# A state-space scan stepped in pairs: 28 of 42 complex rotations taken out of TensorE, two matrices more in their place, and a new order of all instructions

## Chip, cores and metric

One core of one Trainium2 chip. The metric is the time of one execution on the device in microseconds (us); lower is better. The core's engines run beside each other and meet at semaphores: PE (TensorE, matrix products), DVE (VectorE), ACT (ScalarE), POOL (GpSimd) and SP (SyncE, which here issues the DMAs). Each of them works through its own queue in order.

## The reference, cut to what matters

Two independent blocks on 2048 positions of width 448, their outputs set side by side. Block A is attention with 16 heads over a window of 8 positions at a distance of 2; block B is a diagonal complex state model:

```python
qkv = x @ wqkv                                    # A: q, k, v; 16 heads of 28
logits = einsum(q, k[pos - 2*w], w = 0..7) * scale   # masked below position 0
a = einsum(softmax(logits), v[pos - 2*w]) @ wo
...
Lam_bar = exp(exp(log_dt) * Lam)                  # B: 448 complex states
Bu = x @ (((Lam_bar - 1) / Lam)[:, None] * Bmat).T
for t in range(L):
    h = Lam_bar * h + Bu[t]                       # the scan over 2048 steps
y = 2 * real(h_all @ Cmat.T) + x * Dskip
```

## The kernel before

**State of block B.** The 448 complex states lie as 7 groups `g` of 64, real parts on partitions 0 to 63 and imaginary parts on 64 to 127. So a multiplication by a power of `Lam_bar` is a matmul with a 128x128 matrix, a *rotation*: `R[:, g, k]` (built by `rb(k)` on DVE) turns by power k + 1. The 2048 steps are T = 4 residues `j` of 512 chunks, the chunks again even and odd (256 each).

**Steps of block B.** `BU` (line 672) projects x with the transposed B matrix `BT` into a PSUM bank for each (g, j). `BR` (685) adds the state one step earlier, rotated by one power, for j = 1, 2, 3: 21 rotations of 512 columns. `z` (689) evicts each bank to `Z` (for j = 3 the even half to `Z3`); `UP` (697) turns the even half of j = 3 by four steps onto the odd one, and `y` evicts it. `sa`, `sb`, `sd` (716 to 734) scan over the 256 pairs of chunks, on DVE, for two groups at a time (0 and 1, 2 and 3, 4 and 5, 6): turn by tables `tab`, one real scan, turn back. `DN` (737) and `dn` (742) give the even chunks from the odd ones. `H_(j, g)` (748) rotates the state at the chunk's start by j + 1 steps, for j = 0, 1, 2: 21 rotations of 512 columns; `h(j, g)` (755) adds each to `Z`, on DVE from PSUM. `C(j, ct)` (766) then makes a block of 128 output rows: 7 matmuls, one for each g, with `Cw`; `c` (774) adds `x * Dskip`, `oc` stores. The block (j, ct) = (2, 3) is made in two halves, `CH`, `ch`, `oh`. `ca` (ACT) and `cs` (DVE) scale `Cw`; `rk` holds magnitudes.

**Steps of block A.** `XI`, `XA`, `XH` transpose x on PE and `xa`, `xh` evict; `QK`, `QS` (326 to 341) make q and k and `qk`, `qh` evict; `V_`, `v` make v. `P(u, r, ws)` (line 368) multiplies q by four shifted copies of k on DVE, 28 products of 2048 columns; `E_` sums over the head's columns on PE; `lt`, `TR`, `tr`, `sma`, `smb`, `smc` are the softmax; `AL`, `al`, `ad`, `sp` spread the probabilities into bands `PT` through DRAM; `AV`, `av` apply them to v; `W_`, `w`, `ow` are the output projection.

**Who evicts.** The helper `evict` (line 113) takes a PSUM bank to SBUF on ACT where the step in the order ends in ".", and on DVE where it ends in "=". So groups on line 113 hold evictions of many steps; they are told apart by their tiles.

**Order.** Nothing reorders at run time. The string `ORDER` (line 32) is a list of 557 steps; "BU201@12" is the step `BU` with arguments 2, 0, 1 that takes PSUM banks 1 and 2. The loop at line 849 emits the steps in this order, so it is the order on each engine's queue at once, SP's included. The loads of x, `wq` and B at lines 139 to 178 are issued on SP before the list. `WU`, 24 matmuls on zeros and a first `Exp` on ACT, stands second in the list; `BD`, the DMA transposition of B, first. Ahead of the list DVE clears some tiles (lines 116, 224, 226).

Of the kernel before, what the change touches and what calls it, by code (L numbers as in the profile page):

```python
# [17 lines left out]
T = 4  # L18
# [8 lines left out]
SHR = 1.0 - 1e-6  # L27
MAGIC = 12582912.0
# [4 lines left out]
BD WU@0 XI0@12 XI1 xa00= xa01. PP@3 pcopy pa pb pd_ xh0. QS00@4 XH1@5 pc ty5 ty4 pe qk000. pf XA10@6 tf4 tf5 xt1 ts04  # L33
xh1= XA11@7 xa11= xt3 QS10@0 QK021@13 qk010. QK061@24 xa10= QK060 QK020 ts05 pg qh011. QS01@5 qk001. P001 QS11@7
qk020= ts15 qh000. QK041@60 ts25 ty0 QK031@15 P000 qk021. QK030 rb2 tf0 qk030. P020 P021 ts14 QK040 V_100@31 qk011.
P011 qk031. qk041. qh001. ts24 QK050@75 QK051 V_011@02 ts00 ty1 qh010. qk050. V_010 E_00@4 E_02 qk040. tf1 P010 E_01@7
# [26 lines left out]
def kernel(  # L63
# [820 lines left out]
```

## Time and profile before

| | |
|---|---|
| time of the runs shown | median 135.06 us of 3 (134.78 to 135.12) |
| span of the profiled execution, first to last instruction | 132.7 us |
| median less span | 2.3 us |
| busy PE / DVE / ACT / POOL | 125.4 / 116.9 / 89.7 / 19.8 us |
| instructions PE / DVE / ACT | 1068 / 211 / 180 |
| matmuls of `BR` (line 686), 512 columns | 6.3 us in all (20 recorded) |
| matmuls of `H_` (line 752), 512 columns | 6.7 us in all (21) |

The profile gives no time of its own for the profiled execution beyond its span; what lies around the span is taken as the 2.3 us by which the median of the runs exceeds it. A matmul's duration includes its drain, which overlaps the next one; so what a matmul costs in a run of matmuls is the distance from start to start, well below its duration. The same holds for DVE and ACT to a lesser degree. L242 in a row is line 242 of the kernel before. In a timeline or the chain of work the first number is the start and the second the extent, both in us from the span's start; "x3" joins three neighbours. In a table of windows each engine's entry is its busy time in the window, with instructions in brackets.

### The profile page before, as it was taken

How to read it: one execution, taken by the hardware profiler on the slowest of the kernel's cores; microseconds unless marked ns; L12 is line 12 of the kernel's file. 1: busy time of each engine (PE TensorE's matmuls, PEld its weight loads, DVE VectorE, ACT ScalarE, POOL GpSimd, SP SyncE). 2: the span in 40 equal slices, each digit the busy share in tenths (PEclk: the TensorE clock that was granted, in tenths of full speed). 3: DMA queues.
4: the chain of work that ended last, by engine and by line, in shares of the span. 5: the costliest groups of instructions: out<-in, count | busy, mean ns of one | idle time of the engine just before them, and what ended most of it. 6: DMA issues, size and time to landing. Idle time of an engine off the chain costs nothing.

```text
span 132.7 us, 2860 instructions
## 1 busy us (share of the span) xinstructions
PE 125.4 (94%) x1068; PEld 63.4 (48%) x1078; DVE 116.9 (88%) x211; ACT 89.7 (68%) x180; POOL 19.8 (15%) x37
## 2 busy tenths in 40 slices
PE   6987999999999999999999999999999999999990
PEld 6642344344333533435335645955954455555550
DVE  5589999999899999999999798999999996969851
ACT  3396499994578999999899899999999110100000
POOL 6801000000000000035599700000000000000000
PEclk9999999999999999999999999999999999999998
DMA  4897998999989998997849599895513301321543
GB/s 109 201 228 159 304 241 147 152 200 212 263 187 214 208 224 215 380 180 134 223 148 185 199 172 373 187 182 70 175 35 110 104 0 38 105 69 39 182 153 110
DMA packets 45348, 22.62 MB, mean 170 GB/s; under 512 B 33239, under 2 KB 44311, under 8 KB 45335
## 3 DMA queue, kind: packets, MB, share of 16 engines
q1 hardware_dynamic: 45272, 22.45, 73.3%
q8 instruction: 8, 0.13, 0.4%
q14 instruction: 5, 0.04, 0.1%
q10 hardware_dynamic: 63, 0.01, 0.0%
HBM read 11.68 MB, written 6.29 MB: 135 GB/s over the span
## 4 chain that ended last, share of the span: by engine, by line
PE 64%; ACT 15%; DVE 9%; SPq 5%; issue 3%; DMA 2%; POOL 0%
PE ps L242 31%; PE ps L771 14%; PE ps L686 4%; PE ps L380 3%; PE ps L752 3%; SPq L131 2%; ACT ctmp L648 2%; ACT oT L113 2%; SPq L137 2%; ACT kf L113 2%; PE ps L511 2%; DMA wq<-in_A_wqkv_dram 2%; PE ps L498 2%; ACT qf L113 2%; DVE hs L727 1%
## 5 line engine op out<-in xcount | busy, mean ns | idle before, releaser
L368 DVE TENSOR_TENSOR pr<-qf,kf 128x2048 bf16<-128x2048 bf16 x24 | 28.3, 1217 | 0.2 <-ACT kf L113 0.2
L242 PE MATMUL ps<-xbuf,BT 128*128 128x512 bf16 (+1 forms) x108 | 23.1, 379 | 0.7 <-issue 0.6
L242 PE MATMUL ps<-xT,wq 128*128 128x512 bf16 (+1 forms) x92 | 20.9, 380 | 1.4 <-DVE xT L113 0.5
L771 PE MATMUL ps<-Cw,Z 128*128 128x448 bf16 x105 | 21.3, 352 | 0.2
L113 ACT CAST Z<-ps 128x512 bf16<-128x512 f32 (+1 forms) x32 | 15.2, 509 | 1.0 <-PE ps L242 0.6
L113 ACT CAST ya<-ps 128x448 bf16<-128x448 f32 (+1 forms) x14 | 7.3, 547 | 11.5 <-issue 10.9
L771 PEld LDWEIGHTS <-Z 128*128 128x128 bf16 x105 | 10.3, 98 | 10.1 <-issue 0.7
L242 PEld LDWEIGHTS <-BT 128*128 128x128 bf16 (+1 forms) x112 | 8.8, 97 | 12.3 <-issue 3.3
L511 PE MATMUL ps<-wo,oT 128*128 128x448 bf16 x64 | 13.8, 353 | 0.2 <-DVE oT L113 0.2
L242 PEld LDWEIGHTS <-wq 128*128 128x128 bf16 (+1 forms) x96 | 7.6, 97 | 13.1 <-issue 4.0
L757 DVE TENSOR_TENSOR Z<-ps,Z 128x512 bf16<-128x512 f32 x21 | 13.5, 680 | 0.4 <-PE ps L752 0.3
L777 DVE TENSOR_TENSOR xbuf<-ps,xnB 128x448 bf16<-128x448 f32 x15 | 8.9, 619 | 4.6 <-PE ps L771 3.8
L242 PE MATMUL ps<-wq,xT 128*128 128x448 bf16 (+1 forms) x64 | 12.1, 353 | 0.0
L841 POOL MEMSET PT<- 128x4320 f32 x3 | 11.1, 3728 | 1.7 <-ACT Z L113 1.7
L113 ACT CAST kf<-ps 128x512 bf16<-128x512 f32 x12 | 6.9, 593 | 4.0 <-PE ps L242 3.9
L648 ACT ACTIVATE ctmp<-Cw,c2t 64x448 f32<-64x448 bf16 x14 | 9.3, 666 | 0.3
L113 ACT CAST oT<-ps 128x512 bf16<-128x512 f32 x16 | 9.0, 614 | 0.1
L511 PEld LDWEIGHTS <-oT 128*128 128x128 bf16 x64 | 6.1, 98 | 6.1 <-DVE oT L113 0.7
L498 PE MATMUL ps<-PT,v_s 128*32 128x135 bf16 (+1 forms) x256 | 8.3, 298 | 0.0
L242 PEld LDWEIGHTS <-xT 128*128 128x128 bf16 (+1 forms) x64 | 5.0, 97 | 6.4 <-issue 2.6
L498 PEld LDWEIGHTS <-v_s 128*32 128x32 bf16 x256 | 7.0, 112 | 0.4 <-issue 0.4
L113 ACT CAST v_s<-ps 128x448 bf16<-128x448 f32 x14 | 7.0, 549 | 0.0
(153 smaller groups left out, 191.1 us busy)
## 6 DMA issues: line engine op xcount, KB each, us to landing
PT<-pd SPq DMA_DIRECT2D x16, 156.0 KB, 4.0
xnB<-in_B_x_dram SPq DMA_DIRECT2D x2, 896.0 KB
out_dram<-ya SPq DMA_DIRECT2D x16, 112.0 KB, 1.8
out_dram<-xbuf SPq DMA_DIRECT2D x15, 112.0 KB, 1.8
pd<-Ak SPq DMA_DIRECT2D x2, 640.0 KB, 3.7
xbuf<-in_A_x_dram SPq DMA_DIRECT2D x2, 448.0 KB
xnB<-in_B_x_dram SPq DMA_DIRECT2D x4, 224.0 KB, 7.0
xnB<-in_B_x_dram SPq DMA_DIRECT2D x4, 192.0 KB, 4.6
```

The costliest lines, as they stand in the source:

```text
L113: (ACT.copy if e == "A" else V.tensor_copy)(o, i)
L242: PE.matmul(o, l, r, start=(first and i == 0), stop=(not first and i == len(pairs) - 1 and not more[s]))
L368: V.tensor_tensor(t[:], q.unsqueeze(1).to_broadcast((128, 4, 512)), k4, ALU.mult)
L380: PE.matmul(acc[s][32 * i:32 * i + 32], E[:, f, ws, :], t[:, i, :], start=(f == 0 and ws == 0), stop=False)
L498: PE.matmul(p[32 * hh:32 * hh + 32, 128 * bl:128 * bl + n], v_s[:, t, 4 * hg + hh, :], PT[:, t % NS, (4 * hg + hh) // HS, (4 * hg + hh) % ...
L511: PE.matmul(p[:, 0:D], late["oT"][:, b // 4, hg, par, 128 * (b % 4):128 * (b % 4) + 128], late["wo"][:, hg, :], start=(hg == 0), stop=(hg ...
L648: ACT.activation(t[a:a + 64, 0:D], Cw[b:b + 64, g, :], ACTF.Copy, scale=c2t[a:a + 64, g:g + 1])
L686: PE.matmul(pp["z", g, j][:], rot(g, 0), late["Z"][:, g, j - 1, :], start=False, stop=True)
L757: V.tensor_tensor(zz, pp.pop(("h", j, g))[:], zz, ALU.add)
L771: PE.matmul(p[:, 0:D], z, Cw[:, g, :], start=(g == 0), stop=(g == G - 1))
L777: V.tensor_tensor(yo, pp.pop(("c", j, ct))[:, 0:D], xnB[:, ct, j, :], ALU.add)
L841: POOL.memset(late["PT"][:, 4 * i:4 * i + 4].rearrange("p t g n -> p (t g n)").bitcast(F32), 0.0)
```

## The change

Steps now go in pairs (j = 0, 1 and j = 2, 3). The second step of a pair isn't advanced but kept *turned back* by one power: its x is projected with a matrix of its own, `BT[1]` = B turned back by one power, and accumulates onto the first step's sum in the same PSUM bank. What is read out for it is then multiplied with an own output matrix, `Cw[1]` = C turned forward by one power. So within a pair no rotation is needed; `BR` is left once for each group (from pair 0 to pair 1, by two powers), and `H_` once for each group, whose result `h` adds to both steps of the first pair at once.

- New on PE: `BB` (4 matmuls of 128 columns for each group) and `CB` (one of 448) make the two matrices, and ACT evicts them (`bb`, `cb`). `BT[1]` is written in place over `Bn`, once `BD` has read it; `Cw[1]` takes the place of `BT[0]`.
- `BF` and `BX`/`BY` replace `BU`: three full matmuls, and the half-height rest, one for each step. A pair shares a bank, so the second step's matmuls wait for the first step's eviction `z`.
- `DO` and `do` give j = 2 the odd chunks' share beside `DN`'s; `H_` is evicted to SBUF (`hs`), and `h` is one addition of 2 x 512 columns there.
- `R` has three matrices, and the third is first the turn back (`rb2`), then the turn forward (`rb3`). The scans work in place in `Z3`. `w` evicts to the upper half of `xbuf`, in 8 slots where there were 6; `al(3)` uses `Ak0` a second time.
- `ORDER` is new throughout (580 steps) and gives many evictions to another engine: on DVE now 2 `al`, 2 `av`, 2 `ci`, 1 `hs`, 1 `tr`, 6 `z`, 3 `qk`, 2 `v`, 1 `w`, 2 `xa`, 1 `xh`; before 1 `av`, 3 `z`, 3 `qk`, 2 `v`, 3 `w`, 3 `xa`, 1 `xh`. `WU` goes from the second place to the end; `LC`, the loads of C, from behind the four `xt` to ahead of `BD`.

The order's start, its first products, the stretch around the last scan, and its end:

```diff
-BD WU@0 XI0@12 XI1 xa00= xa01. PP@3 pcopy pa pb pd_ xh0. QS00@4 XH1@5 pc ty5 ty4 pe qk000. pf XA10@6 tf4 tf5 xt1 ts04
-xh1= XA11@7 xa11= xt3 QS10@0 QK021@13 qk010. QK061@24 xa10= QK060 QK020 ts05 pg qh011. QS01@5 qk001. P001 QS11@7
...
-sb6 W_41@4 w41. cs2 W_50@7 H_03@5 sd6 DN5@3 dn5 W_60@1 ow31 ca5 W_70@2 ow30 ow41 w60. ow71 h13 cs5 H_11@4 C33@3 w00.
...
-oc10 oc01 oc22 c02 ow51 oc02 CH1@7 ch1 oh1
+XI0@01 XI1 xh0= xa00. PP@2 xa01= QS10@3 pcopy pa XH1@4 xh1. XA10@5 XA11@6 pb QS00@7 xa11. pd_ QK021@01 QK041@24 xa10=
+LC pe ty4 tf4 ty0 QK020 pc qk020= QK040 tf0 QK050@65 qk000. QS11@7 qk040= qk010. QK051 QK031@30 QK030 P001 P000 qk041.
+pf QS01@4 ts04 qk050. V_111@26 ts00 qk051= qk021. qk030. ts10 QK061@51 BD P041 P040 QK060 V_110 P020 qk011. ts20 P021
...
+rb3 AL2@5 cs0 sa0 ts12 z41. ts03 UP2 BF410@6 pm2 pm0 cs6 z51= xd1 sp0 AL3@1 BF611 BR4 BF311 CB6@3 BR5 ts22 al3= ca4
+y2. BX3141 sp1 al2. ts13 BX6151 z63. z33. cb6. AV020@1 sb0 AV000@2 av020. AV011@5 av011. sd0 z42= AV001@3 xd0 z52=
...
+cs5 W_20@2 av100. dn2 DO2 av120. cb0. cb1. H_0@6 sb4 w30. CB5@0 ow11 hs0. W_40@4 w40. CB2@5 sd4 cb2. xd2 W_61@7 W_70@6
+DN3@4 CB3@5 ow00 ow30 ts26 ow31 w61. do2 w70. DN5@3 sa6 dn3 dn5 ow70 sb6 W_51@7 W_41@6 ow10 DO3 w20. do0 H_3@2 cb3.
+sd6 h0 cb5. hs3. ow61 W_60@5 w41. DN4@0 DO5 w60. C32@1 dn4 DN6@2 W_21@6 ow20 do5 w21. do3 dn6 c32 H_2@5 W_50@3 w51.
+DO4 h3 hs2. ow40 DO6 do6 H_5@4 xd3 H_4@6 C31@7 h2 c31 ow41 do4 hs5. hs4. w50= ow21 H_6@1 h5 W_71@5 h4 C33@2 oc31 C21@4
+C22@7 c33 hs6. CH0@6 ch0 h6 C20@0 oc33 c22 CH1@3 C13@1 w71. c20 C10@5 oc32 ch1 C12@2 c21 C03@6 c13 oc21 oh1 ow50 oh0
+c10 oc20 oc10 C00@7 C02@0 oc22 C01@3 c00 c03 c02 C11@4 oc13 oc03 c12 C30@1 oc00 c01 ow60 oc01 WU@5 c11 oc12 c30 oc02
+ow71 oc11 ow51 oc30
```

The steps that are new or changed:

```diff
-    Bn = s2.tile([128, G, 512], BF16, tag="Bn")
+    Bn = keep.tile([128, G, 512], BF16, tag="Bn")
...
-    BT = keep.tile([128, G, 4, 128], BF16, tag="BT")
-    R = keep.tile([128, G, T, 2, 64], BF16, tag="R")
-    Cw = keep.tile([128, G, D], BF16, tag="Cw")
+    BT = [keep.tile([128, G, 4, 128], BF16, tag="BT", name="BT"), Bn.rearrange("p g (f n) -> p g f n", f=4)]
+    R = keep.tile([128, G, 3, 2, 64], BF16, tag="R")
+    Cw = [keep.tile([128, G, D], BF16, tag="Cw", name="Cw"),
+          BT[0].rearrange("p g f n -> p (g f n)")[:, 0:G * D].rearrange("p (g d) -> p g d", g=G)]
...
-    def BR(g, j):
-        PE.matmul(pp["z", g, j][:], rot(g, 0), late["Z"][:, g, j - 1, :], start=False, stop=True)
+    def BB(g):
+        p = pp["bb", g] = ps()
+        for f in range(4):
+            PE.matmul(p[:, 128 * f:128 * f + 128], Bn[:, g, 128 * f:128 * f + 128], rot(g, BACK), start=(f == 0), stop=True,
+                      skip_group_check=True)
+    def bb(g, e):
+        evict(e, BT[1][:, g].rearrange("p f n -> p (f n)"), pp.pop(("bb", g))[:])
+    def CB(g):
+        p = pp["cb", g] = ps()
+        PE.matmul(p[:, 0:D], rot(g, FWD), Cw[0][:, g, :], start=True, stop=True)
+    def cb(g, e):
+        evict(e, Cw[1][:, g, :], pp.pop(("cb", g))[:, 0:D])
...
+    def BF(g, q, s):
+        p, new = zbank(g, q)
+        for f in range(3):
+            PE.matmul(p[:], BT[s][:, g, f, :], xTB[:, q, 4 * s + f, :], start=(new and f == 0), stop=True, skip_group_check=True)
+    def bhalf(g, q, s):
+        p, new = zbank(g, q)
+        r = slice(64 * s, 64 * s + 64)
+        PE.matmul(p[:], BT[s][r, g, 3, :], xTB[r, q, 3, :], start=new, stop=True, skip_group_check=True)
+    def BX(g, q, h, r):
+        bhalf(h, r, 0)
+        bhalf(g, q, 1)
+    def BY(g, q, s):
+        bhalf(g, q, s)
+    def BR(g):
+        p, new = zbank(g, 1)
+        PE.matmul(p[:], rot(g, R2), late["Z"][:, g, 1, :], start=new, stop=True, skip_group_check=True)
...
+    def DO(g):
+        PE.matmul(pp["dn", g][:, N2:], rot(g, R4), late["Z3"][:, g, EV:EV + N2], start=False, stop=True, skip_group_check=True)
+    def do(g):
+        zz = late["Z"][:, g, 2, :]
+        V.tensor_tensor(zz, pp.pop(("dn", g))[:], zz, ALU.add)
-    def H_(j, g):
-        p = pp["h", j, g] = ps()
+    def H_(g):
+        p = pp["h", g] = ps()
...
-    def h(j, g):
-        zz = late["Z"][:, g, j, :]
-        V.tensor_tensor(zz, pp.pop(("h", j, g))[:], zz, ALU.add)
+    def hs(g, e):
+        t = pp["hs", g] = late["sc"].tile([128, NC], BF16, tag="hp", name="hp", bufs=2)
+        evict(e, t[:], pp.pop(("h", g))[:])
+    def h(g):
+        zz = late["Z"][:, g, 0:2, :]
+        V.tensor_tensor(zz, pp.pop(("hs", g))[:].unsqueeze(1).to_broadcast((128, 2, NC)), zz, ALU.add)
...
-            PE.matmul(p[:, 0:D], z, Cw[:, g, :], start=(g == 0), stop=(g == G - 1))
+            PE.matmul(p[:, 0:D], z, Cw[j % 2][:, g, :], start=(g == 0), stop=(g == G - 1))
```

More of the change, by code (lines that the diff above doesn't have):

```diff
@@ L27 @@
 SHR = 1.0 - 1e-6
+FLOOR = 32.0
+R2, R4, BACK, FWD = 0, 1, 2, 2
 MAGIC = 12582912.0
 ORDER = """
[L33 to L36 removed]
```

138 lines of the change are left out of this document (72 added, 66 removed).

## The prediction

> **What bounds the kernel now.** I read the page's first lines and its forty slices, then a table of windows cut where the work changes, then the groups of instructions by shape.
>
> ```profile
> span 132.7 us, 2860 instructions
> ...
> PE   6987999999999999999999999999999999999990
> PEld 6642344344333533435335645955954455555550
> DVE  5589999999899999999999798999999996969851
> ```
>
> PE is full from the fifth slice to the last but one. But DVE is nearly as full until the 31st slice (103 us), and only then has air. The windows give the size:
>
> ```profile
> 14.06:48.00 33.94, 33.57 (x227) 13.67 (x229) 32.75 (x38) 27.03 (x58) 0.00 (x0) 1.00 1.10 212
> 48.00:72.00 24.00, 23.52 (x191) 10.16 (x194) 23.30 (x34) 23.14 (x42) 10.64 (x7) 1.00 0.85 214
> 72.00:102.10 30.10, 29.67 (x426) 18.51 (x427) 27.70 (x60) 28.84 (x58) 3.66 (x2) 1.00 0.71 171
> 102.10:129.65 27.55, 27.31 (x149) 14.24 (x146) 22.46 (x39) 2.32 (x5) 0.00 (x0) 1.00 0.27 86
> ```
>
> Behind the length stand busy PE, weight loads, DVE and ACT. The cuts at 14.06 and 102.10 are DVE's first product `P` and the end of its last scan group `sd6`:
>
> ```profile
> 11.69 0.18 DVE L580 TENSOR_TENSOR co<-cs,rk 128x28 f32<-128x28 f32 x1
> ...
> 14.06 1.22 DVE L368 TENSOR_TENSOR pr<-qf,kf 128x2048 bf16<-128x2048 bf16 x1
> ...
> 101.80 0.29 DVE L734 TENSOR_TENSOR Z<-vv,p 128x256 bf16<-128x256 bf16 x1
> ```
>
> Between these cuts DVE works 32.75 + 23.30 + 27.70 = 83.75 us of 88.04 and is idle 4.3. So two engines bind at once: PE over the whole span, and DVE up to `sd6`. The output stage (`C`, L771) can't begin before the scans are nearly through.
>
> **The change on PE.** Pitches (start to start) come from the chain's pieces, extent over count, and from one run of equal matmuls in the timeline, extent less a duration of 0.22 (L398, the same shape, is a row of 219 ns) over count less one:
>
> ```profile
> 80.21 0.12 PE ps L739
> 80.33 0.65 PE ps L686 x3
> ...
> 107.81 1.32 PE ps L771 x7
> ```
> ```profile
> 8.22 0.84 PE L294 MATMUL ps<-ident,xbuf 128*128 128x128 bf16 x12
> ```
> ```profile
> L398 PE MATMUL ps<-ident,lt 128*128 128x128 bf16 x16 | 1.2, 219 | 0.0
> ```
>
> So 256 columns take 0.11 to 0.12 us, 512 take 0.216, 448 take 0.189, 128 take 0.056. Removed: 14 of the 21 `BR` (L686) and 14 of the 21 `H_` (L752), 28 x 0.216 = 6.05. Added: `BB`, 28 of 128 columns, 1.57; `CB`, 7 of 448, 1.32; `DO`, 7 of 256, 0.76; the halves of B that no longer run two by two (`BY411`, `BY511`, both on the same half of the rows), 0.43. Net 2.0 us less. Changes of matmul shape in PE's order are about as many as before (42 against 44), and `C` is unchanged.
>
> Where the 2.0 lies matters. Ahead of its first `C`, PE loses 14 `BR` and 4 `H_` (3.9 us) and gains 3.9 of the 4.1 us of new work, so it comes there no sooner than now, at about 102.5. Behind it stand 10 `H_` fewer: 2.2 us.
>
> ```profile
> 102.48 1.73 PE L771 MATMUL ps<-Cw,Z 128*128 128x448 bf16 x7
> ```
>
> **The change on DVE.** In total it evens out: 21 additions `h` from PSUM become 7 `do` from PSUM and 7 wider `h` from SBUF, and the new order gives DVE more evictions. But what counts is the work that stands in the order ahead of `sd6`, where DVE is full.
>
> ```profile
> 81.40 1.87 DVE L757 TENSOR_TENSOR Z<-ps,Z 128x512 bf16<-128x512 f32 x3
> ```
> ```profile
> L757 DVE TENSOR_TENSOR Z<-ps,Z 128x512 bf16<-128x512 f32 x21 | 13.5, 680 | 0.4 <-PE ps L752 0.3
> L652 DVE SCALAR_TENSOR_TENSOR Cw<-Cw,c1t,ctmp 128x448 bf16<-128x448 bf16 x7 | 4.7, 675 | 0.2 <-ACT ctmp L648 0.2
> L745 DVE TENSOR_TENSOR Z<-ps,Z 128x256 bf16<-128x256 f32 x7 | 2.8, 416 | 0.5 <-PE ps L739 0.5
> L113 DVE CAST ya<-ps 128x448 bf16<-128x448 f32 x3 | 1.8, 613 | 0.0
> L415 DVE TENSOR_TENSOR attn<-attn,m 128x1024 bf16<-128x1024 bf16 x2 | 1.4, 692 | 0.1
> L113 DVE COPY xT<-ps 128x1024 bf16<-128x1024 bf16 x2 | 1.4, 686 | 1.3 <-PE ps L285 1.3
> ```
>
> Three `h` span 1.87 us, so their pitch is (1.87 - 0.68) / 2 = 0.60: a DVE instruction in a full queue costs its duration less 0.08. By the same rule: 0.53 for an eviction of 448 columns, 0.34 for 256, 0.61 for 1024 of bf16. Ahead of `sd6` come in: `al` 2, `av` 1, `z` of 512 columns 3, `hs` 1, `do` 3, at 0.60 (6.0; casts like `h`); `tr` 1 (0.6); `ci` 2 (ACT's before; 896 elements of bf16, bounds the 0.34 of L745 and twice 0.61, I take the nearest row, `xT`, a little shortened: 0.55 each, 1.1); `cs` 1 (0.6); `dn` 1 (0.3). Out go: `h` 1 for 4 (1.8), `w` 2 (1.1), `xa` 1 (0.6). Net 8.6 - 3.5 = 5.1 us more. Further, `pg` (11.69 to 14.06, 2.4 us) now stands behind the first product, and two `qk` evictions ahead of it, with one `xa` less there: 1.8 us pass from ahead of the first product to behind it. So DVE has 83.75 + 5.1 + 1.8 = 90.65 us between its first product and the end of `sd6`.
>
> The wider `h` (1024 of bf16, one operand repeated) is not in this trace: bounds 0.61 (L415) and 1.2 (two of today's); I take the former, and only one stands ahead of `sd6`.
>
> **When DVE's first product starts.** `qk020` and `qk040` now stand ahead of it on DVE; they wait for PE's `QK041`, `QK020`, `QK040`, in this order. `QK041` needs the last columns of `wq`, whose loads keep their place on SP:
>
> ```profile
> 8.62 2.27 DMA wq<-in_A_wqkv_dram
> ```
>
> 10.9 + 0.22 + 12 x 0.216 + 0.2 (drain, semaphore) + 0.60 (eviction) + 0.1 = 14.6 us, against 14.06 now.
>
> **The sum.** 14.6 + 90.65 = 105.25 for the end of `sd6` if DVE never waits; with all of today's 4.3 us of idle time 109.6. A queue that binds waits less than one that doesn't; today's smallest share is 2.9% (0.70 of 24 us, second window), and I take half of it, 1.4 us: 106.65. `C32` is now PE's first `C`, and its seventh matmul reads group 6, which `sd6` writes. PE would be there at 102.5 + 6 x 0.189 = 103.6, so it waits about 3 us, and behind it in PE's queue stands everything else: from that matmul on 0.19, 14 `C` (18.5), `CH` twice (1.3), 3 `W_` of 4 matmuls (2.3), 4 `H_` (0.9), `DN6` and two `DO` (0.3): 23.5. PE ends at 106.65 + 0.1 + 23.5 = 130.25.
>
> ```profile
> 128.98 0.62 DVE L777 TENSOR_TENSOR xbuf<-ps,xnB 128x448 bf16<-128x448 f32 x1 [0.70 <-DMA out_dram<-xbuf]
> 129.63 0.33 SPq L781 DMA_DIRECT2D out_dram<-xbuf  x1
> 129.65 0.39 DVE L801 TENSOR_TENSOR xbuf<-ps,xnB 128x224 bf16<-128x224 f32 x1
> ```
>
> Today PE ends at 129.65 and 3.1 us follow, with a half addition of 0.39. The new order ends in a whole block (`C30`), 0.62: 3.3 us. Span 133.6. The median of the runs, 135.06, lies 2.3 us over the span of the profiled execution, so 135.9, say **136.0 us**. Equality would need `sd6` done at 105.8, only half a microsecond over the sum without idle time: the margin is narrow, and that sets my chances.
>
> **What I cost at nothing, and its cover.** ACT gets 7 `bb`, 7 `cb` and 6 `hs` and gives up some `z`, `ci`, `al` and `tr`: about 7 us more. Behind 102 us it is idle (2.32 busy of 27.55), but from 48 to 102 it works 52.0 of 54.1 us, and most `bb` and `cb` fall there; cover is that DVE runs later than ACT. Without it a late `smb` or `y` holds DVE, within the 4.3 us above. On SP, `LC` (four loads of `Cr`) moves ahead of `BD` and the four `xt`:
>
> ```profile
> 37.93 8.12 SPq L660 DMA_TRANSPOSE xbuf<-xnB x4
> 46.10 1.11 SPq L266 DMA_DIRECT2D Cr<-in_B_C_re_dram x1
> ...
> 48.45 0.49 SPq L267 DMA_DIRECT2D Cr<-in_B_C_im_dram x1
> ```
> ```profile
> xbuf<-xnB SPq DMA_TRANSPOSE x4, 4.6
> ```
>
> The last `xt` is issued at about 44.0 and lands 4.6 later, 48.6; with 46.10 to 48.94 ahead of it, 51.4. PE's first `BF` would come at about 50 and waits some 1.5 us. DVE is the later engine there, so I cost it at nothing; without that cover it is 1.5. `WU` goes to the end, behind `C30`: 24 x 0.056 = 1.3 us beside the last addition and store.
>
> `WU` leaves the start, and that is where something speaks against the change:
>
> ```profile
> 1.05 2.74 PE L260 MATMUL ps<-wz 128*128 128x128 bf16 x24 [1.05 <-DVE wz L116]
> 3.66 0.82 PE L285 MATMUL ps<-ident,xbuf 128*128 128x128 bf16 x6
> ```
>
> The first 24 take 2.74 / 24 = 0.11 each, the transposes at 3.66 0.82 / 6 = 0.14, those at 8.22 0.84 / 12 = 0.07 (extents with the last one's drain): PE starts at half pace and is at full pace 4 to 7 us after its first matmul, though the granted clock stands at 1.00. Without `WU` the first matmul is at 3.66, so full pace comes 2.6 us later, by 8.3 to 10.8. Until `wq` is there at 10.9 that hides in PE's waits.
>
> The Trainium skill, "TensorE: Matmul & The Clock Gate" (Part 1, the HAM clock gate), says that the array runs at half clock until a free-running window of about 3.4 us was busy. The trace's two paces agree; by the rule a missed window would cost 3.4 us more at half pace.
>
> **Rivals.** *Half pace lasts.* If full pace comes only after 10.9, the 12 matmuls ahead of `qk040` take up to 2.6 us longer, and DVE's first product and the end move by as much; half of them, 1.3: 137.2 us. For it: the first matmuls stand 2.6 us later. Against: 7 us of waits lie there. Chance 0.08. (The skill's page above is the rule behind it.)
>
> *DVE waits as today.* The 4.3 us of idle time come back, 2.9 more than I took, by ACT (52.0 of 54.1) or the transfers: 138.8 us. Chance 0.12.
>
> *PE stays the bound, and the kernel is faster.* If DVE's items ahead of `sd6` are some 2 us cheaper than counted (`ci` at its lower bound, the casts at 0.5) and DVE waits for nobody, `sd6` ends near 103.3 and the 2.0 us less come through: 132.7 - 2.0 + 0.2 + 2.3 = 133.2. It decides from `sd6` below 105.4. For it: the 22.46 of 27.55 us behind `sd6` show where air is, and the total of DVE is unchanged. Against: the count. Chance 0.25, mostly near 134.
>
> *The two cancel*: `sd6` between 105.4 and 106.2, 135.1 us, chance 0.13. That the rotations don't go can't be: they are not issued.
>
> **How the numbers follow.** Forecast 0.42 (135.5 to 138), half pace 0.08, DVE waiting 0.12, cancel 0.13, PE bound 0.25. 0.3% is 0.4 us, about what a measurement here can tell from no change. So slower 0.62, same 0.13, faster 0.25. Range: 133.8, which takes in most of the faster case, to 139.3, which takes in the late ones.
>
> **What would show it.** In the new profile: DVE's first product at 14 to 16 us; DVE nearly without gaps until `sd6`, which ends behind 105; PE waiting some us at its first `C`, for DVE; matmuls at twice the pitch until 8 to 11 us; PE idle under 2 us ahead of the first `BF`. I am wrong if `sd6` ends before 105, if PE has no wait at its first `C`, or if PE waits for something else (the probabilities in `PT`, ACT's evictions) more than for DVE.

## The result and the profile after

| | before | changed |
|---|---|---|
| median of the runs | 135.09 us (4 runs, 134.78 to 135.24) | 147.14 us (4 runs, 144.40 to 148.51) |
| ratio | | 1.0735, 95% interval 1.0657 to 1.0812 |
| span of the profiled execution | 132.7 us | 146.4 us |
| its own time | not given | 148.39 us |

The change makes the kernel slower by 7.4%; the forecast was 136.0, in a range from 133.8 to 139.3. The ratio leaves out runs with a lowered clock, so it lies under that of the medians; the profiled execution ran at a mean granted clock of 0.965, and a good part of that has a cause in the kernel, shown below.

The head of the changed kernel's profile page and three rows of its slices:

```profile
span 146.4 us, 2897 instructions
...
PE   0899999999599998996299994999599999999993
...
DVE  6446999995999999999994999499979999973451
...
PEclk9999999999999999999659999599999999999999
```

Before, PE had a 9 in every slice from the fifth to the last but one. Now there are holes: slices 11, 19 and 20, 25 and 29, and twice the granted clock falls with a hole or behind it. The chain that ended last, first of before, then of the changed kernel, by engine:

```profile
PE 64%; ACT 15%; DVE 9%; SPq 5%; issue 3%; DMA 2%; POOL 0%
```
```profile
DVE 30%; PE 27%; DMA 24%; SPq 12%; issue 4%; DVEq 0%
```

Before, one engine carried most of the chain. Now it is passed between DVE, PE, transfers and the queue that issues them: a chain of waits. One row of the table of windows for each kernel, from DVE's first product to the end of `sd6` (columns: window, length, then busy PE, PEld, DVE, ACT, POOL, and the granted clock); before, then changed, where the second row runs on to the end of PE's work:

```profile
14.06:102.10 88.04, 86.76 (x842) 42.34 (x850) 83.75 (x130) 79.01 (x155) 14.30 (x7) 1.00 0.90 198
```
```profile
16.23:118.60 102.37, 91.28 (x867) 44.17 (x873) 93.27 (x157) 84.74 (x172) 13.19 (x6) 0.95 0.79 166
```
```profile
118.60:142.50 23.90, 23.82 (x133) 12.89 (x133) 16.92 (x30) 5.14 (x9) 0.00 (x0) 1.00 0.25 78
```

DVE is busy 93.27 of 102.37 us. The waits that matter there (engine, line, what it waited for: us in total, times, longest):

```profile
PE ps L716 <- DVE Z L116: 4.1, 1, 4.1
...
PE ps L501 <- DMA PT<-pd: 3.5, 2, 1.8
...
DVE oT L116 <- PE ps L501: 1.9, 1, 1.9
DVE Cn L116 <- DMA Cr<-in_B_C_im_dram: 1.8, 1, 1.8
...
PE ps L387 <- DVE pr L371: 1.7, 1, 1.7
```

The largest has its origin on an engine that the prediction gave no cost. DVE's timeline of the changed kernel, then POOL's:

```profile
67.38 3.82 DVE L622 TENSOR_SCALAR kM<-iot,fT 128x256 f32<-128x256 f32 x1
71.30 0.42 DVE L623 SCALAR_TENSOR_TENSOR fr<-kM,fr 128x256 f32<-128x256 f32 x1
71.69 0.69 DVE L116 CAST Z<-ps 128x512 bf16<-128x512 f32 x1
```
```profile
67.36 7.47 POOL L905 MEMSET PT<- 128x4320 f32 x2
```

`kM`, the first instruction of step `tf2`, takes 0.35 us elsewhere and 3.82 here. POOL began clearing a third of `PT` 0.02 us earlier, and the two memsets are 3.74 each: `kM` ends with the first of them. Behind it on DVE stood `z02`, for which PE waited 4.1 us. What PE did next:

```profile
72.44 1.44 PE L716 MATMUL ps<-xbuf,Bn 128*128 128x512 bf16 x3 [4.14 <-DVE Z L116]
73.67 1.49 PE L716 MATMUL ps<-xbuf,BT 128*128 128x512 bf16 x3
74.95 1.49 PE L716 MATMUL ps<-xbuf,Bn 128*128 128x512 bf16 x3
```

From 73.67 to 74.95 are three matmuls, 0.427 each, twice the 0.216 of before: PE fell to half pace. So the two engines lost time one after the other over one instruction of 0.35 us.

In the same terms as the prediction's sum, from the profiled executions (us; "work" is DVE's busy time between first product and end of `sd6`):

| kernel | first product | work | idle | end of `sd6` | behind it | span |
|---|---|---|---|---|---|---|
| before | 14.06 | 83.75 | 4.3 | 102.1 | 30.6 | 132.7 |
| forecast | 14.6 | 90.65 | 1.4 | 106.65 | 26.95 | 133.6 |
| changed | 16.23 | 89.8 + 3.47 blocked | 9.1 | 118.6 | 27.8 | 146.4 |
| `e1_stt` | 15.25 | 90.15 | 8.1 | 113.5 | 27.9 | 141.4 |
| `f1_stt_ci0` | 15.86 | 90.06 | 6.0 | 111.96 | 27.8 | 139.8 |
| `f6_chain` | 15.70 | 90.34 | 5.2 | 111.2 | 27.8 | 139.0 |
| `f8_pm` | 16.11 | 88.44 | 5.8 | 110.37 | 28.6 | 139.0 |
| `h1_less_dve` | 16.52 | 83.27 | 9.9 | 109.68 | 28.2 | 137.9 |
| `b5_sp0_late` | 13.80 | 83.94 | 7.1 | 104.87 | 30.6 | 135.5 |

### The profile page after: what moved, and what is told of

Its sections match the earlier page's. It is cut to its first block, busy times and chain, and to the rows that moved or that the text cites. A ratio compares the mean times of both kernels' runs of the same rounds, so it can differ in the third digit from the quotient of the medians.

```text
span 146.4 us, 2897 instructions
## 1 busy us (share of the span) xinstructions
PE 128.6 (88%) x1083; PEld 64.3 (44%) x1092; DVE 120.0 (82%) x213; ACT 96.4 (66%) x196; POOL 18.7 (13%) x36
## 4 chain that ended last, share of the span: by engine, by line
DVE 30%; PE 27%; DMA 24%; SPq 12%; issue 4%; DVEq 0%
PE ps L837 13%; DVE pr L371 11%; DMA PT<-pd 8%; DMA xbuf<-in_A_x_dram 7%; PE ps L501 6%; SPq L175 4%; DMA Bn<-in_B_B_im_dram 4%; PE ps L716 4%; DMA Cr<-in_B_C_im_dram 3%; DVE kM L622 3%; SPq L470 3%; DMA pd<-Ak 2%; DVE R L639 2%; SPq L140 2%; SPq L180 1%
## 5 line engine op out<-in xcount | busy, mean ns | idle before, releaser
L371 DVE TENSOR_TENSOR pr<-qf,kf 128x2048 bf16<-128x2048 bf16 x24 | 27.8, 1220 | 0.1
L716 PE MATMUL ps<-xbuf,Bn 128*128 128x512 bf16 x39 | 12.3, 417 | 4.3 <-DVE Z L116 4.1
L116 ACT CAST Z<-ps 128x512 bf16<-128x512 f32 (+1 forms) x29 | 13.1, 503 | 3.8 <-PE ps L721 3.8
L245 PE MATMUL ps<-wq,xT 128*128 128x448 bf16 (+1 forms) x64 | 12.9, 353 | 0.0
L905 POOL MEMSET PT<- 128x4320 f32 x3 | 11.2, 3740 | 5.2 <-DVE z L429 5.2
L837 PE MATMUL ps<-BT,Z 128*128 128x448 bf16 x56 | 11.5, 352 | 0.0
L716 PE MATMUL ps<-xbuf,BT 128*128 128x512 bf16 x39 | 11.2, 399 | 0.2
L116 ACT CAST oT<-ps 128x512 bf16<-128x512 f32 x15 | 8.2, 604 | 2.6 <-PE ps L501 2.6
L837 PE MATMUL ps<-Cw,Z 128*128 128x448 bf16 x49 | 9.8, 352 | 0.0
L116 ACT CAST xbuf<-ps 128x448 bf16<-128x448 f32 x15 | 7.7, 543 | 2.3 <-issue 2.1
L716 PEld LDWEIGHTS <-Bn 128*128 128x128 bf16 x42 | 4.0, 102 | 9.1 <-issue 6.2
```

What stands on the lines that cost most here:

```text
L116: (ACT.copy if e == "A" else V.tensor_copy)(o, i)
L245: PE.matmul(o, l, r, start=(first and i == 0), stop=(not first and i == len(pairs) - 1 and not more[s]))
L371: V.tensor_tensor(t[:], q.unsqueeze(1).to_broadcast((128, 4, 512)), k4, ALU.mult)
L716: PE.matmul(p[:], BT[s][:, g, f, :], xTB[:, q, 4 * s + f, :], start=(new and f == 0), stop=True, skip_group_check=True)
L837: PE.matmul(p[:, 0:D], z, Cw[j % 2][:, g, :], start=(g == 0), stop=(g == G - 1))
L905: POOL.memset(late["PT"][:, 4 * i:4 * i + 4].rearrange("p t g n -> p (t g n)").bitcast(F32), 0.0)
```

## Experiments

Times are medians of four runs (ten for `b3_wu_end` and `b4_wu_last`), beside 134.9 to 135.2 us of the kernel before on the same chip. A ratio is that to the kernel before, run beside it. Edits of the order are shown as steps.

### The blocked instruction

**`e1_stt`**, the changed kernel with `kM` in another form:

```diff
-        V.tensor_scalar(kM, iot[:], fT[:, g:g + 1], MAGIC, ALU.mult, ALU.add)
+        V.scalar_tensor_tensor(kM, iot[:], fT[:, g:g + 1], cols[:, 5:6].to_broadcast((128, N2)), ALU.mult, ALU.add)
```

> The changed kernel, with only the first instruction of tf (kM) as scalar_tensor_tensor in place of tensor_scalar; the order is untouched. In the changed kernel's profile one of the seven kM took 3.82 us instead of 0.35, and it ended as POOL's clearing of a PT block (3.74 us, begun 0.02 us before it) ended. Theory 'port': DVE's tensor_scalar and POOL's memset shut each other out, and this form doesn't need what they share; then no kM lasts over 0.5 us, PE's 4.3 us wait behind the last scan-independent products and the half pace after it go, and the span falls by 4 to 7 us to 139 to 143. Rival 'chance': the long kM is something else (a late input); then one kM stays long and the time within 1% of the changed kernel's 147.1.

Measured 143.75 us (142.82 to 144.38). The group of `kM` on DVE (count, busy us, mean ns):

```profile
L623 DVE SCALAR_TENSOR_TENSOR kM<-iot,fT,cols 128x256 f32<-128x256 f32 x7 | 3.3, 478 | 0.0
```

All seven take 0.48 us, although POOL clears `PT` beside two of them (67.23 to 74.57, `kM` at 67.48 and 73.29): this form isn't blocked by the memset. What the block with what followed it was worth is less certain: 3.4 us by the medians, 1.3 by the ratios (1.0735 against 1.0642, 1.0576 to 1.0707, so the intervals overlap). Only one execution of the changed kernel was profiled, its time near the longest of the four, and 0.02 us decided there; whether `kM` is blocked in all of them isn't shown.

**`b1_collide`**, the kernel before with `tf2` a few steps later:

```diff
-... BU100 tf2 z10. BU010@51 z22. pm2 xd0 ad0 ...
+... BU100 z10. BU010@51 z22. pm2 xd0 tf2 ad0 ...
```

> The kernel before, with only tf2 moved two places later, behind xd0, so that its kM (0.35 us, at 64.4 us, 0.2 us ahead of POOL's clearing of PT) comes at about 65.4, inside the first clearing (64.6 to 68.3). Theory 'port': this kM lasts about 3 us, until the clearing ends, DVE slips by 2.6 us and the time grows by 1 to 2.6 us over 135.1. Rival 'chance': the kM stays at 0.35 and the time within 0.4 us of 135.1.

Measured 136.75 us, ratio 1.0141 (1.0082 to 1.0199).

```profile
65.51 3.04 DVE L613 TENSOR_SCALAR kM<-iot,fT 128x256 f32<-128x256 f32 x1
```
```profile
64.71 11.12 POOL L841 MEMSET PT<- 128x4320 f32 x3 [1.69 <-ACT Z L113]
```

The block is made at will in the kernel before: `kM` begins 0.8 us into a memset of 3.7 and waits out its rest. In the original order `kM` was at 64.38 and the memset at 64.59; it had missed by 0.2 us. The Trainium skill, "SBUF — State Buffer" (Who interferes with whom), says that DVE's `tensor_scalar` in its two-port mode and GpSimd share a pair of ports, and that whoever starts first holds it for the whole instruction. The three traces agree, in the order of starts (0.02 us decided in the changed kernel) and in the length.

### The load of C

**`e4_ci0_late`**, the changed kernel with the eviction `ci0` behind a later product:

```diff
-tf1 ci0= qk111. ... lt01 P100 V_000
+tf1 qk111. ... lt01 P100 ci0= V_000
```

> The changed kernel with one eviction-like copy, ci0 on DVE, moved behind P100 (two rotations' set-up and three products later). In the changed kernel DVE stands 1.8 us in front of it because the loads of C land only at 36.8 us, and PE then waits 1.9 us for the product queued behind. Theory 'queue': both waits go, 1.5 to 1.9 us less at that place; how much reaches the end depends on the kM collision, 0 to 4 us. Rival: DVE catches up anyway and the end doesn't move (under 0.5 us).

Measured 143.69 us (143.25 to 144.63), ratio 1.0652 (1.059 to 1.0714), with `kM` still blocked twice (1.35 and 3.19 us). In the changed kernel DVE's row was

```profile
36.89 0.40 DVE L116 COPY Cn<-Cr 128x896 bf16<-128x896 bf16 x1 [1.77 <-DMA Cr<-in_B_C_im_dram]
```

`ci0` was ACT's before and is DVE's now; `LC`, moved ahead of `BD`, was issued from 31.02 on, and its loads landed just ahead of 36.89. Behind `ci0` stood a product, and PE waited 1.7 us for it.

**`f1_stt_ci0`**, both edits:

> The changed kernel with two edits together: kM as a three-operand instruction on DVE (as in the first experiment, 143.75 us), and ci0, the eviction of the loads of C, behind the product P100 instead of ahead of qk111. Theory (DVE's count of work ahead of sd6 was right, and what was lost is idle time with separate causes, so the causes add): DVE's 2.7 us of waiting for Cr goes, the stall of TensorE near 37 us with it, and the time falls by 2.3 to 2.7 us to about 141.2. Rival (one chain sets everything, from the softmax over the probabilities' transfers to the first AV, and time won ahead of it is lost again in front of it): AV waits for PT longer by the same amount, time 143.4.

Measured 141.23 us (140.66 to 141.89), ratio 1.0421 (1.0335 to 1.0507): the theory's number. The two causes together are worth 5.9 us by the medians and 4.2 by the ratios. They are separate, in that either edit still gains 2.5 us when the other is in place (3.0 by the ratios); but either alone gained 3.4 by the medians and only 1.1 to 1.3 by the ratios, so how much belongs to each stays open.

### The pace at the start

**`e3_wu_start`**, the changed kernel with `WU` first in the order instead of near the end:

> The changed kernel with WU moved from the end back to the first place of the order. Theory 'pace': full pace comes at 5.6 us instead of 13.2, DVE's first product at about 14.9 instead of 16.2, and that 1.3 us goes through the full DVE queue to the end: 1 to 1.5 us less, unless the kM collides otherwise. Rival 'hidden': the first product still waits for the last piece of wq (10.9 us) and nothing is gained, under 0.4 us. Whether kM collides with POOL here is open; with the collision the time is near 146, without it near 141.

Measured 147.53 us, ratio 1.0911 (1.0849 to 1.0973): no gain, rather a loss. The first product came at 15.61 instead of 16.23, not at 14.9, since PE fell back to half pace: the granted clock was 0.50 from 9 to 11 us, behind waits of 0.66 and 0.92 us for its inputs. `kM` was blocked here too (2.63 us). Why the time rose is open.

**`b3_wu_end`** and **`b4_wu_last`**, the kernel before without `WU` at its start:

```diff
-BD WU@0 XI0@12 ...
-... c22 oc10 oc01 ... CH1@7 ch1 oh1
+BD XI0@12 ...
+... c22 oc10 WU@0 oc01 ... CH1@7 ch1 oh1      (b3_wu_end)
+... c22 oc10 oc01 ... CH1@7 WU@0 ch1 oh1      (b4_wu_last)
```

> The kernel before, with WU (24 matmuls on zeros) moved from the second place in the order to near the end, where the changed kernel has it; nothing else. Theory (the start at half pace costs): full pace comes at about 13 us instead of 5.6, the first product comes 1.2 to 1.6 us later than 14.06, and the time rises to 136.0 to 136.6. Rival (the wait for wq until 10.9 us hides it): first product at 14.1 to 14.4, time 134.9 to 135.2.

Measured 136.87 us. The first product came at 14.07, as before, so the theory's step is wrong. `WU`'s 1.3 us stood ahead of the last half block, a fault of this run's place for it; hence the second one.

> The kernel before, with WU behind its last matmuls, so that its 1.3 us stand beside the last addition and store (in the run with WU near the end they stood ahead of the last half block). Theory (the start at half pace costs, but little, since the first product came at the same time): 135.4 to 136.0 us. Rival one (no cost): 135.05. Rival two (it costs as in the earlier run, 136.9): 136.5 and more.

Measured 135.16 us, ratio 1.0003 (0.9982 to 1.0025): no cost. PE does run at half pace until about 12 us, but the first product, at 14.04, stands behind DVE's `pg` and doesn't come later.

### What holds the first AV

**`f2_pt`**: `f1_stt_ci0` with `tf3` behind `al1`, `ad2 sp2` behind `al2`, `z52= z42=` behind `z33.`, and `BF411 BF511` ahead of `AV020`.

> As the kernel before in this list, and the transfers of the probabilities eased: tf3 (0.9 us of DVE) behind al1, ad2 and sp2 right behind al2 and ahead of the AVs (sp2 fills slots that nobody has read yet), the evictions z52 and z42 ahead of sb0, and with them the six matmuls BF411 and BF511 ahead of the first AV. Theory (idle time by separate causes): DVE had 3.7 us of idle time between 80 and 104 us with the probabilities behind them; some 2.5 us of it go, time about 138.7, and TensorE waits for PT under 1.5 us in all instead of some 7. Rival (DVE's work itself is too long, and idle time only moves): the waits for PT shrink, but sd6 ends less than 0.7 us sooner, time 140.5 or more.

Measured 141.83 us (141.49 to 143.46), so the rival's. PE's wait for `PT` fell from 4.7 to 1.5 us, but DVE now waited 1.5 us for PE's half-height matmuls ahead of `z52`, PE 1.4 for DVE's evictions ahead of `BF411`, and `sd6` came no sooner (112.2 against 111.96).

**`f3_act`**: the same with five evictions given to ACT (`al3= z31= hs1= av031= qk051=` end in "." instead).

> As the kernel before in this list, and five evictions given from DVE to ACT (al3, z31, hs1, av031, qk051; 0.6 us each on DVE, 3.0 in all). Theory (DVE is the engine that sets the end of sd6, nearly without gaps by now): sd6 ends 2 to 3 us sooner and the time falls by as much, about 136. Rival one (TensorE or the transfers set it by now): no change, 138.5. Rival two (ACT is as full as DVE from 48 to 102 us): its queue gets late, the AVs and scans wait for it, 139.5.

Measured 142.61 us (142.27 to 143.54): no gain over `f2_pt`, as in the first rival; the numbers set beforehand, all below this one, started from the 138.7 that `f2_pt` didn't reach. DVE's work ahead of `sd6` fell by 2.9 us and its idle time rose from 6.1 to 9.6.

**`g1_fill`**: `f1_stt_ci0` and one step more.

```diff
+    def FI():
+        p = ps()
+        for _ in range(12):
+            PE.matmul(p[:], rot(0, R2), late["Z"][:, 0, 1, :], start=True, stop=True)
-... cb6. AV020@1 ...
+... cb6. FI@1 AV020@1 ...
```

> The kernel with kM in the three-operand form and ci0 late (141.23 us), and 12 matmuls of 512 columns more, right ahead of the first AV, whose result nobody reads: 2.6 us of TensorE's work, about what 12 of the 28 rotations cost that the change took out. Theory (TensorE has 3.1 us of waiting there, so the removed rotations saved nothing at that place): time unchanged within 0.5 us, AV's wait for PT falls from 3.1 to about 0.5 us, and the granted clock behind it stays up. Rival (TensorE binds, or the wait has other causes): time up by 2 to 2.6 us, 143.5.

Measured 141.03 us (140.85 to 141.63).

```profile
81.40 2.76 PE L688 MATMUL ps<-Z,R 128*128 128x512 bf16 x12
84.22 2.02 PE L502 MATMUL ps<-PT,v_s 128*32 128x135 bf16 x60
```

Twelve rotations' worth of matmuls, 2.76 us, fit into the wait and cost nothing. So rotations taken out ahead of the first `AV` saved nothing there.

**`f4_soft`**: `f1_stt_ci0` with `rb1 tf2 tf3` behind `al1=`, `cs2` behind `smc1`, `ad2 sp2` behind `al2.`; **`f5_soft_wu`**: the same with `WU` first.

> The changed kernel with kM in the three-operand form and ci0 late (141.23 us), and the way to the probabilities shortened: rb1, tf2 and tf3 (2.9 us of DVE) go behind al1, cs2 (0.6) behind smc1, and ad2 and sp2 stand right behind al2. Nothing else moves and no work goes. Theory (what holds the first AV is the chain of the softmax on DVE, the way through DRAM and the landing; TensorE reaches it earlier than in the kernel before because its rotations are gone): AV's wait of 3.1 us for PT goes nearly, the second one of 1.5 too, sd6 ends 2 to 4 us sooner, time 137.5 to 139. Rival (DVE and TensorE wait for each other's next step in turn, whatever the transfers do): time 140.5 to 141.5.

Measured 143.58 us (143.44 to 145.46), worse by 2.3 than without the edit and above both the theory and the rival. In its waits:

```profile
ACT ctmp L658 <- DVE attn L433: 2.3, 1, 2.3
```

`ca0` on ACT waited for a buffer until the end of `smc1`, behind which `cs2` now stood, and PE waited 2.2 us for the evictions behind `ca0`; and `sp2`, waiting on SP for its load, stood ahead of `ad3`, so that the second `AV` waited 2.9 us for `PT`. Two of the moves had put a wait at the head of another queue.

> As the kernel before in this list, with WU back at the start. Theory (half pace at the start costs): first product 0.5 to 1.3 us sooner than the 15.9 us of the kernel with ci0 late, and the time falls by as much. Rival (the loads and the queue order set the first product, since TensorE falls back to half pace in its waits anyway): first product within 0.3 us, time within 0.4 us.

Measured 145.71 us (144.51 to 146.17), 2.1 more than `f4_soft`, which neither the theory nor the rival had. The first product came at 15.11, but in `f4_soft`, without `WU` at the start, it had come at 15.29: so there was hardly a sooner start whose worth could be read. PE's wait for `PT` was 4.4 us instead of 2.9, and DVE waited 1.5 us for the loads of C again; why is open.

**`f6_chain`**, without those two moves, and **`f7_xd`**, with two scalings of x besides:

```diff
-... CD2 rb1 CD1 ... z21. tf2 smb1 ... BR2 tf3 z61. ... al1= BX3040 ... ad2 av010. ... ca1 sp2 cs3
+... CD2 CD1 ... z21. smb1 ... BR2 z61. ... al1= rb1 tf2 tf3 BX3040 ... ad2 sp2 av010. ... ca1 cs3
-... z51= xd1 sp0 ... AV001@3 xd0 z52= ... h2 c31 ... w71. c20      (f7_xd)
+... z51= sp0 ... AV001@3 z52= ... h2 xd1 c31 ... w71. xd0 c20      (f7_xd)
```

> The changed kernel with kM in the three-operand form and ci0 late (141.23 us), and of the failed shortening of the way to the probabilities only the parts that put no wait into another queue: rb1, tf2 and tf3 (2.9 us of DVE) behind al1, cs2 stays where it was, and sp2 stands right behind ad2, so ahead of sp3 but behind ad3. Theory (the first AV is held by softmax, DRAM and landing; the failed run lost its gain to ca0, which waited on ACT for a buffer, and to ad3, which waited on SP behind sp2): AV's waits for PT of 3.1 and 1.5 us go to under 1 us together, sd6 ends 2 to 3.5 us sooner, time 138 to 139.3. Rival (engines wait for each other in turn, and the gain ends elsewhere): 140.7 to 141.7.

Measured 141.39 us (139.45 to 141.94): the rival's, although PE's wait for `PT` fell from 4.7 to 1.9 us.

> As the kernel before in this list, and xd0 and xd1 (1.08 us of DVE each) moved behind sd6, to just ahead of the additions that read them (c20 and c31). Theory (with the waits gone DVE's work ahead of sd6 sets the end): 1.5 to 2.2 us less than the kernel before in this list, about 136.5. Rival (TensorE and the transfers set it by now): less than 0.5 us.

Measured 140.95 us (140.38 to 142.22): the rival's again. 1.9 us less work ahead of `sd6`, which came 0.5 us sooner.

### Which engine's own work binds

Both kernels are `f6_chain` with work left out: **`h1_less_dve`** drops the steps `xd0` to `xd3` and `cs0` to `cs6` from the order; **`h2_less_pe`** has

```diff
-        for hg in range(4):
+        for hg in range(1):
```

in `W_`.

> The kernel with the shortened chain (141.39 us; three-operand kM, ci0 late, rb1, tf2, tf3 and sp2 moved), with work left out on DVE: no multiplication of x by Dskip (xd) and no scaling of C (cs). The output isn't the reference's; ahead of sd6 7.4 us of DVE's work go, on no other engine. Theory (DVE's own work sets the end of sd6): sd6 ends 6 to 7 us sooner and the time falls to 134.5 to 135.5. Rival (DVE and TensorE hold each other in turn, so that no engine's work alone sets it): the time falls by 1 to 4 us, 137.5 to 140.5.

Measured 139.96 us (138.58 to 140.64), ratio 1.0333 (1.0247 to 1.0418): 1.4 us by the medians, 0.7 by the ratios, for 7 us of DVE's work. The rival's. The window row, first product to `sd6`:

```profile
16.52:109.68 93.16, 87.60 (x863) 43.31 (x870) 83.27 (x147) 84.35 (x171) 13.05 (x6) 1.00 0.83 179
```

> The same kernel with the chain shortened (141.39 us), with work left out on TensorE: the output projection takes one matmul for each block instead of four (the sum over the head groups is cut short, so the output isn't the reference's). Ahead of sd6 36 matmuls of 448 columns go (6.8 us), behind it 12 (2.3 us). Theory (ahead of sd6 DVE's work sets the end, behind it TensorE's): the time falls by 2.3 us and by less than 1 us more, 138 to 139.3. Rival (DVE and TensorE hold each other in turn): it falls by 4 to 7 us, 134.5 to 137.5.

Measured 139.76 us (139.13 to 141.96), ratio 1.0315 (1.0229 to 1.0401): 1.6 us less by the medians, 1.0 by the ratios, for some 9 us of PE's work. The rival's 4 to 7 us didn't come; the time lies just above the theory's range, and the theory's half about DVE has just fallen. The profiled execution was the longest of the four, and with 139.9 us of span no shorter than that of `f6_chain` (139.0), so it doesn't show where the gain of the others lies:

```profile
15.68:112.47 96.79, 83.77 (x825) 39.98 (x832) 90.43 (x157) 84.56 (x171) 13.05 (x6) 0.99 0.86 178
```

Compare `f6_chain`:

```profile
15.70:111.20 95.50, 88.32 (x866) 43.48 (x872) 90.34 (x157) 84.65 (x171) 13.05 (x6) 1.00 0.83 180
```

Take 7.1 us from DVE (90.34 to 83.27) and the window shrinks by 2.3; take 4.6 busy us from PE (88.32 to 83.77) and in the one execution seen it doesn't shrink. Neither engine's work alone sets the window; most of what is taken away comes back as waiting.

### The transfers of PT

In `f6_chain` SP's waits name a third party:

```profile
SPq L471 <- POOL PT L906: 2.7, 1, 2.7
```

The new order clears the block that `sp0` fills (`pm0`) last of the three and has `sp0` behind `ad1`: all eight transfers are issued from 74.85 on, right after the last memset (67.48 to 74.82). Before, `sp0` was issued from 68.43 on.

**`f8_pm`** is `f7_xd` with that undone, **`b5_sp0_late`** the kernel before with that put in:

```diff
-... z13. pm1 pm4 ... BF310@0 ad1 ... pm2 pm0 cs6 ... z51= sp0 AL3@1      (f8_pm)
+... z13. pm0 pm1 pm4 ... BF310@0 sp0 ad1 ... pm2 cs6 ... z51= AL3@1      (f8_pm)
-... BU211 pm0 z01. ... z23. sp0 BR33 ... BU410@76 pm1 y2. ... z53. sp1      (b5_sp0_late)
+... BU211 pm1 z01. ... z23. BR33 ... BU410@76 pm0 y2. ... z53. sp0 sp1      (b5_sp0_late)
```

> The kernel with the chain shortened and xd0, xd1 late (140.95 us), and POOL's clearing of PT in another order: the block that sp0 fills (pm0) first instead of last, and sp0 ahead of ad1 on SP instead of behind it. No work is added or taken. Theory (the first AV is held by PT's transfers, which in the new order stand behind the last of three memsets and behind ad1, where the kernel before issues sp0 seven us sooner): all of PT's first eight transfers are issued by about 77.7 instead of 79.3, AV's first wait goes, sd6 and the time come 1 to 2 us sooner, 139 to 140. Rival (the engines' mutual waiting is elsewhere): within 0.5 us of 140.95.

Measured 140.88 us (140.08 to 141.74): the rival's. The first wait went (0.28 us left), and the chain that ended last then ran elsewhere:

```profile
81.26 0.49 ACT oT L116
81.78 5.08 DMA pd<-oT
...
89.92 5.31 DMA PT<-pd
95.23 0.84 issue
96.07 0.41 PE ps L502 x7
```

That is the second round: `al2`, late on ACT, goes to DRAM in 5.1 us and comes back in 5.3, and the second `AV` starts at 96.07 (96.68 in `f6_chain`), hardly sooner although the first one no longer waits.

> The kernel before with the changed kernel's handling of PT: the memset of the block that sp0 fills (pm0) stands last of the three instead of first, and sp0 behind ad1 instead of ahead of it. Nothing else moves. Theory (as for the kernel before in this list): the eight transfers stand in one row behind the last memset, TensorE waits 2 to 3 us for PT at its first AV, which it reaches at 82.1 without a wait now, and the time rises by 1 to 2.5 us to 136 to 137.5. Rival (DVE's scans cover it): 135.0 to 135.4.

Measured 137.83 us (137.44 to 139.48), ratio 1.023 (1.0163 to 1.0298), the theory's side and 0.3 us beyond its range:

```profile
85.10 2.14 PE L498 MATMUL ps<-PT,v_s 128*32 128x135 bf16 x64 [2.17 <-DMA PT<-pd]
```

In the kernel before, the same handling costs 2.9 us. There the first `AV` starts at 82.10 without a wait, because the transfers are issued by 77.7 and PE has matmuls until then.

No version of the changed kernel with all of its work came under 139.4 us in any run; the kernel before stays the fastest.

## Why the prediction was right in sign and wrong in size

**Right: the side, and the count.** DVE's work ahead of `sd6` was counted at 90.65 us; it is 89.8 without the blocked part, and 90.1 to 90.3 in the runs without the block. PE's work behind `sd6` was put at 23.5, and it took 23.9. That the gain on PE stands behind `sd6` held too: from there to the end the span went from 30.6 to 27.8 us.

But the side was in good part luck. The forecast had the kernel slower because DVE has 6.9 us more work ahead of `sd6`. `h1_less_dve` has 83.27 us of it, less than the 83.75 of the kernel before, and is still slower than that kernel by 3.3%: most of the slowdown that stays has another cause.

**Wrong: "A queue that binds waits less than one that doesn't; I take half of it, 1.4 us."** This is the step that failed. DVE had 9.1 us of idle time and 3.47 of blocked time, 11.2 us more than taken, of the 12.8 by which the span was missed (146.4 against 133.6). The shortest of the four runs, not profiled, has a span of 142.5 and still misses by 8.9. The step rested on DVE's being the engine that binds, read off from its share of busy time. `h1_less_dve` shows for the changed kernel with its two faults mended (`f6_chain`) that it isn't: with 7.1 us less of work `sd6` came 1.5 us sooner. In its place the runs show three things.

1. 3.47 us of block by POOL and half pace behind it (1.3 us of the time by the ratios, 3.4 by the medians, `e1_stt`; cause made at will in `b1_collide`).
2. A wait for the loads of C, 1.8 us on DVE, 2.5 us of the time with the block gone (`f1_stt_ci0` against `e1_stt`) and 1.1 by the ratios with it (`e4_ci0_late`). The prediction did count `ci0` as DVE work and `LC` as moved, but asked only who is late behind `LC`, not whether its own reader has come sooner than the load.
3. 5 to 6 us of waits in turn that stay when both are gone, the order of the 4.3 us of before. The rival "DVE waits as today" had this (138.8 us, chance 0.12), and 0.42 went to the forecast that assumed it away. Beside 139.0 to 139.8 us of span in `f1_stt_ci0` to `f8_pm` the forecast of 133.6 is still 5.4 to 6.2 short: 3.8 to 4.6 of idle time, 1.1 to 1.5 of first product, 0.9 to 1.7 behind `sd6`, less 0.3 to 2.2 of work.

What exactly keeps those 5 to 6 us isn't settled. Shown is what doesn't do it alone: DVE's work, PE's, the first transfers of `PT`, evictions on DVE. ACT's work (84.65 of 95.50 us busy in `f6_chain`) was never taken away, so that rival is untested. `f8_pm` gives the next link, ACT's `al2` and the second way through DRAM; that it is the last one is only read from its chain, not tried.

**Wrong: `C32` waits about 3 us for `sd6`.** The row of its seven matmuls, and that of the next block:

```profile
117.40 1.62 PE L837 MATMUL ps<-BT,Z 128*128 128x448 bf16 x7
...
121.66 1.49 PE L837 MATMUL ps<-BT,Z 128*128 128x448 bf16 x7
```

1.62 us where the next block's seven span 1.49: it waited 0.13. PE did not arrive at 102.5, as predicted, but at 117.4, since it had lost the time earlier: in its waits at 68, 89 and 103 us (4.1, 1.8 and 1.7) and at half pace behind the first two. That PE has no wait at its first `C` was one of the prediction's own signs of being wrong.

**Wrong by a term: the first product, 14.6 against 16.23.** DVE's rows:

```profile
14.23 0.69 DVE L116 CAST qf<-ps 128x512 bf16<-128x512 f32 x1 [1.12 <-PE ps L245]
14.84 0.34 DVE L622 TENSOR_SCALAR kM<-iot,fT 128x256 f32<-128x256 f32 x1
15.28 0.43 DVE L623 SCALAR_TENSOR_TENSOR fr<-kM,fr 128x256 f32<-128x256 f32 x1
15.63 0.68 DVE L116 CAST qf<-ps 128x512 bf16<-128x512 f32 x1
16.23 1.22 DVE L371 TENSOR_TENSOR pr<-qf,kf 128x2048 bf16<-128x2048 bf16 x1
```

Between the two evictions stands `tf0`, 0.8 us, plain in the order (`qk020= QK040 tf0 ... qk040=`), which the sum had not. The rest is the half pace on PE ahead of `qk020`, which lasted until about 12 us here (the next matmul starts at 11.88, so these three take 0.47 each, beside 0.216):

```profile
10.46 1.49 PE L340 MATMUL ps<-xT,wq 128*128 128x512 bf16 x3
```

How long it lasts differs from one execution to the next. In `e1_stt`, whose order is the same, `qk020` was evicted at

```profile
13.11 0.69 DVE L116 CAST qf<-ps 128x512 bf16<-128x512 f32 x1 [0.23 <-PE ps L246]
```

and with `WU` at the start (`f5_soft_wu`) at 12.98, hardly sooner. In the table above the first product of the changed kernel and its versions, all without `WU` at the start, comes between 15.25 and 16.52. **The rival "half pace lasts"** thus came true for the first product of the profiled execution, but not for every one, and gave nothing for the time: `WU` at the start gained nothing in `e3_wu_start` and `f5_soft_wu`, and its lack cost nothing in `b4_wu_last`.

**Costed at nothing:** ACT's `bb` and `cb` held PE up by 0.5 us in `f1_stt_ci0` and never DVE; the cover was good. `LC` ahead of `BD` held no `BF` up either: the first one ran at 52.87 without a wait. `sp0` and the memsets were not looked at, though both stand in the diff of the order; in `f8_pm` that cost under 0.5 us, since other waits lay beside it, and in `b5_sp0_late` 2.9.

## What to carry over

Where several in-order engines are each some 85 to 98% busy, the sum of one engine's work is a lower bound, and today's idle share is the fairer guess for the rest; assuming it away needs a run such as `h1_less_dve`. When an order is rewritten, go through each queue, POOL's and SP's too, for what now stands next to or behind what: an instruction of 0.35 us that starts 0.02 us after a long memset, a reader that has come ahead of its load, transfers behind the last of three memsets. A gain on an engine that waits further on is only worth what is left of it there: put the work back as a filler and see whether the time changes.

## What the runs showed of the hardware that was not expected

- DVE's `tensor_scalar` of 128x256 f32 (0.35 us) stood still for 3.47, 2.69 and 2.28 us (changed kernel, `b1_collide`, `e3_wu_start`) behind POOL's memset of 128x4320 f32 (3.7 us each); the three-operand form beside the same memset took 0.48, with seven of seven within 0.01 us in `e1_stt`. It isn't free of POOL altogether: begun less than 0.1 us after POOL's copy of `wq` (0.6 us) it took 0.83 us in `f2_pt` and 0.87 in `f8_pm`.
- PE's pace fell to half after single waits in the middle of the kernel. The granted clock in the 8 us that hold the wait or follow it: 0.66 after 4.1 us, 0.79 after 3.06 (`f1_stt_ci0`), 0.79 after 2.2 (`f4_soft`), 0.85 after 2.17 (`b5_sp0_late`), 0.79 after 1.84 (changed kernel, at 91.1); 1.00 beside a wait of 0.9 (`f8_pm`), 1.53 (`f1_stt_ci0`) or 1.67 (changed kernel, at 104.2). The Trainium skill, "TensorE: Matmul & The Clock Gate" (Part 1, the HAM clock gate), names an idle window of some 3.4 us for the fall; here 1.84 us was enough. The length of a wait alone doesn't decide: at the start the clock stood at 0.50 from 9 to 11 us behind waits of 0.66 and 0.92 (`e3_wu_start`), and at 1.00 behind 0.66 and 1.41 (`f5_soft_wu`). Rows of the table of windows of the changed kernel, with the clock as the third number from the end:

```profile
72.00:80.00 8.00, 7.56 (x38) 2.65 (x37) 6.04 (x11) 3.86 (x8) 2.83 (x1) 0.66 0.01 2
80.00:88.00 8.00, 7.88 (x65) 3.73 (x67) 7.58 (x14) 7.92 (x16) 0.00 (x0) 1.00 1.03 202
88.00:96.00 8.00, 6.10 (x139) 4.47 (x139) 6.00 (x12) 6.48 (x15) 0.00 (x0) 0.79 0.77 210
```

- The changed kernel's four runs spread from 144.4 to 148.5 us, those of the kernel before from 134.8 to 135.2 (in later comparisons 134.7 to 136.9). Whether the block, which 0.02 us decided, makes the difference isn't shown.
